# Three heads instead of two in a block-diagonal tile: the recurrent state of an mLSTM cell

## The chip, the cores and the metric

The kernel runs on one core of a Trainium2 chip. The metric is device time in microseconds (us), the median over several executions; lower is better. The engines meant below are TensorE (PE; its weight loads are listed apart as PEld), VectorE (DVE), ScalarE (ACT), GpSimd (POOL) and SyncE (SP), which here only issues transfers.

## The reference

An mLSTM cell is followed by a feed-forward block. There are 4 batches (B), 8 heads (H), 768 time steps (S) and a head dimension of 40 (D). The cell is a recurrence over time with a matrix state C and a vector state n for each batch and head:

```
m_new  = max(f + m, i)
f_stab = exp(f + m - m_new);  i_stab = exp(i - m_new)
C = f_stab * C + i_stab * v k^T
n = f_stab * n + i_stab * k
y = sigmoid(o) * (C q) / max(|n q|, 1)
```

The outputs y of all heads, 8 x 40 = 320 numbers per time step, form the rows x of a matrix of 3072 tokens. The block then computes `h = x @ w_in` (320 x 2048), `g = h - tanh(h)` and `g @ w_out` (2048 x 320). All of it is float32.

## The kernel before, in words

**Units and chunks.** Time is cut into 6 chunks of 128 steps. A unit is one chunk of one batch, all 8 heads of it, so there are 24 units (NU); unit n has chunk c = n // 4 and batch b = n % 4. Two units make a group of 256 tokens for the feed-forward block, which takes its 16 blocks of 128 hidden features in pairs.

**What a unit does.** The recurrence is written chunk by chunk. Within a chunk, a head's output is a masked product of scores with values (`scores`, then a mask on VectorE that writes P, then `intra`: one matmul per head, `ph<-vs,P`). What came before the chunk enters through the state: `inter` multiplies q by the state and starts the accumulation in the same PSUM tile `ph`. Units of the first chunk (0 to 3) have no state yet, so 20 of the 24 units have products with q. `gate` divides and applies the sigmoid, `turn` transposes the result with three matmuls (`px`), and ScalarE copies it to xT, the input of the feed-forward block. `update` forms k^T times the scaled values (`pc`), and `keep_state` adds the old state and multiplies by the decay on VectorE: new = (pc + old) * decay. The last four units update nothing, so 20 units have updates too. The values have a 41st column (D1 = D + 1) that carries the normaliser n along.

**The tile of two heads.** The state of a batch is a tile of 80 rows (TOP = 2 * D, line 283; the tiles at line 498). Heads 2j and 2j + 1 form pair j. Rows 0 to 39 belong to the even head, rows 40 to 79 to the odd one, and the columns hold 41 for each head. The two diagonal blocks are the two states; the other two blocks must be zero. `update` computes the whole square of 80 by 82 in one matmul, cross terms included, and the decay tile eT (line 333) removes them: it holds exp of the summed log decays in the diagonal blocks and zeros elsewhere. `states` (line 422) fills eT with two exponentials and one multiplication by zero on ScalarE, in each of three calls. The summed log decays come from a matmul with a matrix `ones` of TOP columns (line 319). Because the state is block-diagonal, one matmul of `inter` with q of two heads stacked in 80 rows (the tile q2) gives the outputs of both heads side by side: 128 rows of time, 2 x 41 columns.

In the trace a tile named q2 is shown as q. The float32 matmuls stand there as two records each, each with a weight load of its own. The first operand after the arrow in `ph<-state,q` is the one that is streamed, the second the one that is loaded as weights: for `inter` q2 is loaded (128 columns) and the state is streamed (82 columns); for `update` k is loaded (80 columns) and the scaled values are streamed (82 columns).

**Loads.** `load_unit` (line 287) issues a unit's transfers on SP, in order: kz and qz (q and k for the scores, two transfers each, one per half of the partitions), v, k, o and, if there is a state, q2 (two transfers, one for each 40 rows). k, q2 and most others have 3 buffers, so unit n's transfer waits until unit n - 3 has used its buffer.

**What sets the order of the work.** Every instruction on TensorE, VectorE and ScalarE is pinned behind the one written before it. For units 0 to 11 and the first feed-forward items a planner (class Plan, line 157) decides the order: each piece of work has an engine, an estimated time, what it comes after and a rank; the planner takes what can start first by its own clock, and of equals that with the lower rank. In it the second part of a unit (`inter` and `intra`) is four pieces, one per pair, of 0.43 us each with a state and 0.29 without; the updates of a unit are one piece of 0.55 us in which all four matmuls stand in a row (line 918 and the lines after). From unit 12 on the order is fixed by spreading: `cell_slot` (line 621) lists the steps of a unit, and `merge` (line 822) places them at even distances among the matmuls of the feed-forward block. So `inter`, `intra` and `update` stand there one at a time between wide matmuls (`ph_up`, 256 columns streamed, and `pS`, 160).

At the end of the kernel a conditional part (line 1237) repeats everything in a more general way if some values exceed a bound. In this execution it isn't entered: none of its instructions is in the trace.

Of the kernel before, what the change touches and what calls it, by code (L numbers as in the profile page):

```python
# [59 lines left out]
L = 128  # L60
# [18 lines left out]
def kernel(  # L79
# [200 lines left out]

    TOP = 2 * D

    ld = {}

    def load_unit(n, names=("kz", "qz", "v", "k", "o", "q2"), queue=nc.sync):
        c, b = divmod(n, B)
        t = ld.setdefault(n, {})
        for name in names:  # L290
            if name in ("kz", "qz"):
                t[name] = load.tile([128, HH, L], FP, name=name, tag=name, bufs=3)
                for i in range(2):
                    src = kT if name == "kz" else qT
                    queue.dma_start(out=t[name][i * HALF:i * HALF + D], in_=src[b, c, :, slice(i, H, 2)])
            elif name != "q2":
                src, bufs = {"v": (v, 3), "k": (k, 3), "o": (o_gate, 4)}[name]
                t[name] = load.tile([L, H, D], FP, name=name, tag=name, bufs=bufs)
                queue.dma_start(out=t[name], in_=src[b, c])
            elif c:  # L300
                t["q2"] = load.tile([TOP, HH, L], FP, name="q2", tag="q2", bufs=3)
                for i in range(2):
                    queue.dma_start(out=t["q2"][i * D:(i + 1) * D], in_=qT[b, c, :, slice(i, H, 2)])

    for n in range(2):
        load_unit(n, ("kz",))
# [23 lines left out]
    make_identity(nc, ident)  # L330
    V.memset(ones, 1.0)

    eT = const.tile([TOP, NU, HH, 2], FP, name="eT")
    G.memset(eT, 0.0)

    G.memset(upto, 1.0)
# [46 lines left out]
    def gate_columns(c0, c1, bank):  # L383

        cs = slice(c0, c1)
        some = CHUNKS.index(c0)
        least = sums[:, NS + some:NS + some + 1]

        def turned(i, row):
            p = bank(i, [L, NT, BH])  # L390
            for c in range(c0, c1):
                T.transpose(p[:, c, :], row[:, c * L:(c + 1) * L], ident[0:BH, 0:BH])
            return p[:, cs]

        def sums_of(i, w):
            p = bank(i, [w.shape[1], NT, BH])
            T.matmul(p[:, cs].rearrange("p c n -> p (c n)"), w, lfT[:, cs].rearrange("p c n -> p (c n)"),
                     start=True, stop=True)
            return p[:, cs]

        got = {}

        def forget():
            got["lf"] = turned(0, lf)

        def admit():
            got["i"] = turned(1, i_sb)

        def since():
            got["since"] = sums_of(0, upto)  # L410

        def whole():
            got["whole"] = sums_of(1, ones).rearrange("p c (b j two) -> p (c b) two j", two=2, j=HH)

        us = slice(c0 * B, c1 * B)

        def bounded():
            V.tensor_single_scalar(inv[:, cs], got["since"], 2 * DEEP, op=OP.max)
            V.tensor_reduce(out=least, in_=inv[:, cs].rearrange("p c n -> p (c n)"), axis=mybir.AxisListType.X, op=OP.min)
            V.tensor_single_scalar(least, least, TINY / DEEP, op=OP.mult)  # L420

        def states():
            A.activation(out=eT[:, us, :, 1], in_=got["whole"][:, :, 1, :], func=AF.Exp)
            A.activation(out=eT[0:D, us, :, 0], in_=got["whole"][0:D, :, 0, :], func=AF.Exp)
            A.mul(out=eT[0:D, us, :, 1], in_=eT[0:D, us, :, 1], mul=0.0)

        return {
            "forget": forget, "admit": admit, "since": since, "whole": whole,
            "lf": lambda: V.tensor_copy(out=lfT[:, cs], in_=got["lf"]),
            "i": lambda: A.activation(out=ei[:, 1, cs], in_=got["i"], func=AF.Exp),  # L430
            "bounded": bounded,
            "inverse": lambda: A.activation(out=inv[:, cs], in_=inv[:, cs], func=AF.Exp, scale=-1.0),
            "over": lambda: V.tensor_tensor(out=ei[:, 0, cs], in0=ei[:, 1, cs], in1=inv[:, cs], op=OP.mult),
            "states": states}
# [60 lines left out]

    part = [const.tile([L, DM], FP, name=f"part{i}") for i in range(FIRST * GT)]
    ys = [const.tile([L, DM], FP, name=f"ys{i}") for i in range(2)]
    state = [[const.tile([TOP, HH, 2, D1], FP, name=f"state{b}_{i}") for i in range(2)] for b in range(B)]

    un = {}  # L500

    def pair(t, j):

        return t[:, 2 * j:2 * j + 2].rearrange("p two d -> p (two d)")

    def arrive(n):
        t = un.setdefault(n, {})
# [59 lines left out]
    def inter(n, j):  # L567
        t = un[n]
        if "ph" not in t:
            t["ph"] = small([L, H, D1], "ph")  # L570
        if t["c"]:
            T.matmul(pair(t["ph"], j), t["qs"][:, j, :], pair(state[t["b"]][t["c"] % 2].rearrange("p j two d -> p (j two) d"), j), start=(j == 0), stop=False,
                     skip_group_check=True)

    def intra(n, h):
# [16 lines left out]
    def update(n, j, at_once=True):  # L592
        t = un[n]
        if j == 0:
            t["pc"] = small([TOP, HH, 2, D1], "pc")
        T.matmul(t["pc"][:, j].rearrange("p two d -> p (two d)"), pair(t["k"], j), pair(t.get("vs_end", t["vs"]), j), start=True, stop=True)
        if j == HH - 1 and at_once:
            keep_state(n)

    def keep_state(n):  # L600
        t = un[n]
        old, new = (state[t["b"]][(t["c"] + i) % 2].rearrange("p j two d -> p (j two) d") for i in range(2))
        pc = t["pc"].rearrange("p j two d -> p (j two) d")
        decay = eT[:, n].rearrange("p j two -> p (j two)").unsqueeze(2).to_broadcast([TOP, H, D1])
        if t["c"]:
            V.tensor_tensor(out=new, in0=pc, in1=old, op=OP.add)
        V.tensor_tensor(out=new, in0=new if t["c"] else pc, in1=decay, op=OP.mult)
# [13 lines left out]
    def cell_slot(s, o):  # L621
# [8 lines left out]
            begin(s)  # L630
        if o is None:
            return [(0.0, lambda: prepare(s))]
        for d in range(HH):
            steps.append((0.22 if o >= B else 0.0, lambda d=d: inter(o, d)))
            steps += [(0.22, lambda h=h: intra(o, h)) for h in (2 * d, 2 * d + 1)]
        steps.append((0.0, lambda: gate(o)))
        steps += 5 * pause
        if o + B < NU:
            steps += [(0.18, lambda j=j: update(o, j)) for j in range(HH)] + 4 * pause
        steps += [(0.11, lambda j=j: turn(o, j)) for j in range(NK + 1)] + 2 * pause  # L640
        if s is not None:
            steps.append((0.0, lambda: prepare(s)))
# [275 lines left out]
    def plan_unit(n, rank):  # L918
# [41 lines left out]
        def second_part(j):  # L960
            banks[:] = [held["small"]]
            inter(n, j)
            for h in (2 * j, 2 * j + 1):
                intra(n, h)

        for j in range(HH):
            op = plan.add("T", 0.43 if c else 0.29, lambda j=j: second_part(j), [op] if op else [*u["mask"], u["prep"], u["column"], *before, *of(n, "q2") * (c > 0)], rank,
                          take=() if op else [("small", held)], give=[("P", held)] if j == HH - 1 else ())
        u["second"] = op
        u["gate"] = plan.add("V", 1.5, lambda: gate(n), [op, u["open"], *of(n - 2, "turn")], rank, give=[("small", held)])  # L970

# [1 line left out]

        def updates():
            banks[:] = [held_c["small"]]
            for j in range(HH):
                update(n, j, at_once=False)

        def turns():
# [198 lines left out]
    def begin_any(n):  # L1178
# [7 lines left out]
                             op0=OP.mult, op1=OP.add)  # L1186
        t["decays"] = True
        if t["c"]:
            t["qs"] = att.tile([128, HH, L], FP, name="qs", tag="P", bufs=4)[0:TOP]
            for i in range(2):  # L1190
                spread(t["qs"][i * D:(i + 1) * D], g_rows, n, slice(i, H, 2))
            V.tensor_tensor(out=t["qs"], in0=t["qs"], in1=t["q2"], op=OP.mult)

    def keep_any(n):

        t = un[n]
        old, new = (state[t["b"]][(t["c"] + i) % 2] for i in range(2))
        decay = eT[:, n].unsqueeze(3).to_broadcast([TOP, HH, 2, D1])

        own = att.tile([TOP, HH, 2, D1], FP, name="own", tag="P", bufs=4)  # L1200
        V.memset(own, 1.0)
        V.memset(own[0:D, :, 1], 0.0)
        G.affine_select(out=own[:, :, 0], in_=own[:, :, 0], compare_op=OP.is_ge, fill=0.0, base=D - 1,
                        pattern=[[0, HH], [0, D1]], channel_multiplier=-1)
        V.tensor_tensor(out=own, in0=t["pc"], in1=own, op=OP.mult)
        if t["c"]:
            V.tensor_tensor(out=new, in0=old, in1=decay, op=OP.mult)
            V.tensor_tensor(out=new, in0=new, in1=own, op=OP.add)
        else:
            V.tensor_copy(out=new, in_=own)  # L1210
# [26 lines left out]
    with tc.If(nc.values_load(again, min_val=0, max_val=128,  # L1237
# [18 lines left out]
        for g in range(NG):  # L1256
            for n in range(g * GT, (g + 1) * GT):
# [3 lines left out]
                un[n]["vs_end"] = scaled(n, 1, "vs_end", 1)  # L1261
                un[n]["column"]()
                halves(scores(n))
                for j in range(HH):
                    inter(n, j)
                for h in range(H):
                    intra(n, h)
                gate(n)
                if n + B < NU:
                    for j in range(HH):  # L1270
                        update(n, j, at_once=False)
                    keep_any(n)
                for j in range(NK + 1):
# [58 lines left out]
```

## Time and profile before

| what | value |
|---|---|
| median of 3 runs | 565.8 us (565.06 to 565.92) |
| the profiled execution, first to last instruction (its span) | 559.5 us |
| TensorE clock granted, mean | 0.997 |
| TensorE busy; weight loads | 546.4 us; 461.2 us |
| VectorE busy | 346.0 us |
| ScalarE busy | 179.3 us |
| records of products with q, `ph<-state,q` | 160 |
| records of updates, `pc<-vs,k` | 160 |
| first and last product with q start | 59.4 us; 484.0 us (weight load; matmul) |
| first and last update start | 34.1 us; 406.4 us (weight load; matmul) |

The profile is of one execution, whose own time is known only as its span; what lies between it and the median of the runs, 6.3 us, is what precedes the first and follows the last instruction, together with the difference of one execution from another. A group of instructions in it is shown as line, engine, operation, output <- inputs, partitions x elements of each form and how many; then busy time in us and the mean of one in ns; then the idle time just before them and what ended it. Line 129 is the helper through which all matmuls go, line 133 the same for transposes, line 106 that for VectorE and ScalarE; so tiles, not lines, tell operations apart. In a timeline a row is start in us, length in us, engine, line, operation and tiles, and how many were merged. A matmul's length holds its latency, so the pace is read from one start to the next. A row of the table by stage is a stretch (from:to and its length), then busy us and count of PE, PEld, DVE, ACT and POOL, the clock, the busy share of the DMA engines and GB/s.

### The profile page before, as it was taken

Reading aid. Unit: us, or ns where it says so; the run is one execution under the profiler, and the core shown is the slowest. Engines: PE = TensorE matmul, PEld = TensorE weight load, DVE = VectorE, ACT = ScalarE, POOL = GpSimd, SP = SyncE. Lnnn points to the kernel's source line nnn. Section 1 sums busy time; section 2 is a strip of 40 time slices with the busy share of each in tenths; the row PEclk is TensorE's granted clock in tenths of the full one; section 3 lists DMA queues with packets and bytes.
Section 4 is the critical chain, followed back from the end, with each engine's and each line's share of the span. In section 5 each row is a group of like instructions: output and inputs, shape, how many; then the busy total and the mean of one; then the engine's idle time right before and its main releaser. Section 6 shows DMA issues by size and latency. Waiting matters only on the chain.

```text
span 559.5 us, 9108 instructions
## 1 busy us (share of the span) xinstructions
PE 546.4 (98%) x3460; PEld 461.2 (82%) x3460; DVE 346.0 (62%) x754; ACT 179.3 (32%) x441; POOL 34.3 (6%) x67
## 2 busy tenths in 40 slices
PE   7999999999999999999999999999999999999995
PEld 4767978787877777798898999989989989988873
DVE  4699888989854335767656647547556546553421
ACT  2344652443432312322232142133123123131321
POOL 6142030500000000000000000000000000000000
PEclk9999999999999999999999999999999999999998
DMA  7786353632210001201202112121110000000000
GB/s 217 216 260 215 119 171 91 183 113 94 83 36 1 0 1 54 77 23 49 84 25 60 57 41 69 48 83 49 58 37 13 0 25 2 2 25 0 25 0 29
DMA packets 40194, 38.21 MB, mean 68 GB/s; under 512 B 3856, under 2 KB 37712, under 8 KB 40144
## 3 DMA queue, kind: packets, MB, share of 16 engines
q1 hardware_dynamic: 32712, 22.49, 13.7%
q0 software_dynamic: 3296, 10.82, 6.1%
q10 hardware_dynamic: 4136, 4.26, 2.2%
q8 instruction: 29, 0.48, 0.3%
q14 instruction: 21, 0.17, 0.1%
HBM read 33.62 MB, written 3.93 MB: 67 GB/s over the span
## 4 chain that ended last, share of the span: by engine, by line
PE 95%; DVE 2%; DMA 1%; issue 0%; SPq 0%; ACT 0%
PE ph_up L129 40%; PE pS L129 20%; PE po L129 15%; PE ph L129 10%; PE ps L129 4%; PE pc L129 2%; PE px L133 2%; DMA kz<-in_kT 1%; DVE gt L106 1%; PE awake L129 0%; DVE P L106 0%; DVE w_e L106 0%; DVE w_in L106 0%; PE gate L129 0%; DVE den L106 0%
## 5 line engine op out<-in xcount | busy, mean ns | idle before, releaser
L129 PE MATMUL ph_up<-xT,w_in 128*128 128x256 f32 (+1 forms) x1152 | 248.9, 394 | 1.2 <-DVE gt L106 0.8
L129 PEld LDWEIGHTS ph_up<-xT,w_in 128*128 128x128 f32 (+1 forms) x1152 | 170.4, 190 | 34.3 <-issue 13.0
L106 ACT ACTIVATE z<-ph_up 128x512 f32<-128x512 f32 (+1 forms) x100 | 57.1, 576 | 283.4 <-issue 153.3
L106 DVE SCALAR_TENSOR_TENSOR gt<-ph_up,z 128x512 f32<-128x512 f32 (+1 forms) x100 | 63.4, 663 | 92.8 <-ACT z L106 92.5
L129 PE MATMUL po<-w_out,gt 128*128 128x320 f32 x320 | 93.9, 439 | 0.0
L129 PEld LDWEIGHTS po<-w_out,gt 128*128 128x128 f32 x320 | 58.5, 190 | 25.7 <-issue 5.0
L106 DVE TENSOR_TENSOR P<-ps,upto 128x512 f32<-128x512 f32 x48 | 31.6, 684 | 70.4 <-PE ps L129 70.4
L106 ACT ACTIVATE q<-z,tiny 128x512 f32<-128x512 f32 (+1 forms) x100 | 64.8, 701 | 0.0
L106 DVE SCALAR_TENSOR_TENSOR gt<-q,gt 128x512 f32<-128x512 f32 (+1 forms) x100 | 63.2, 662 | 2.0 <-ACT q L106 2.0
L129 PEld LDWEIGHTS ph<-vs,P 128*128 128x128 f32 x384 | 60.5, 202 | 4.7 <-issue 1.2
L129 PE MATMUL ph<-vs,P 128*128 128x41 f32 x384 | 59.7, 272 | 0.0
L129 PE MATMUL pS<-wT,s 128*128 128x160 f32 x336 | 52.0, 301 | 0.0
L129 PEld LDWEIGHTS pS<-wT,s 128*128 128x128 f32 x336 | 47.4, 190 | 0.0
L129 PE MATMUL pS<-w_out,gt 128*128 128x160 f32 x224 | 43.7, 315 | 0.0
L129 PEld LDWEIGHTS pS<-w_out,gt 128*128 128x128 f32 x224 | 32.7, 191 | 4.0 <-issue 3.0
L129 PE MATMUL ps<-qz,kz 40*128 40x128 f32 x384 | 30.1, 297 | 1.2 <-DMA kz<-in_kT 1.2
L129 PE MATMUL ph<-state,q 80*128 80x82 f32 x160 | 31.2, 276 | 0.0
L129 PEld LDWEIGHTS ps<-qz,kz 40*128 40x128 f32 x384 | 27.4, 205 | 4.1 <-issue 2.7
L129 PEld LDWEIGHTS ph<-state,q 80*128 80x128 f32 x160 | 26.4, 191 | 2.7 <-issue 0.7
L448 POOL DMA_DIRECT2D w<-in_moe_w_in x40 | 22.5, 566 | 52.9 <-DVE w_e L106 43.2
L106 ACT COPY xT<-px 128x384 f32<-128x384 f32 x24 | 11.4, 476 | 39.6 <-PE px L133 39.6
L129 PEld LDWEIGHTS pc<-vs,k 128*80 128x80 f32 x160 | 17.9, 150 | 4.8 <-DVE state L106 0.7
(90 smaller groups left out, 443.5 us busy)
## 6 DMA issues: line engine op xcount, KB each, us to landing
w<-in_moe_w_out POOLq DMA_DIRECT2D x16, 320.0 KB, 3.6
kz<-in_kT SPq DMA_DIRECT2D x48, 80.0 KB
o<-in_o_gate SPq DMA_DIRECT2D x24, 160.0 KB
k<-in_k SPq DMA_DIRECT2D x24, 160.0 KB
out<-ob ACTq DMA_DIRECT2D x24, 160.0 KB
qz<-in_qT SPq DMA_DIRECT2D x44, 80.0 KB
v<-in_v SPq DMA_DIRECT2D x22, 160.0 KB
q<-in_qT SPq DMA_DIRECT2D x40, 80.0 KB
```

The costliest lines, as they stand in the source:

```text
L106: i = method(*args, **kwargs)
L129: return cls.keep(nc.tensor.matmul(*args, **kwargs))
L133: return cls.keep(nc.tensor.transpose(*args, **kwargs))
L448: queue.dma_start(out=to[rows, cols], in_=part)
```

## The change

The heads are grouped in threes: heads 0 to 2, 3 to 5, and 6 and 7. The state tile has 120 rows and its columns are head by head as before; the blocks on the diagonal of each trio (40 rows by 41 columns) are the states. `inter` becomes three matmuls: q of up to three heads stacked in 120 rows (80 for the last) as weights, and 123, 123 and 82 columns of state streamed. `update` becomes three matmuls that load 120 columns of k each. For the last trio there are only two heads, so the tile of k is widened to nine heads; its transfer reads 360 numbers per row, the last 40 of which belong to the next row, and the rows of `pc` that come from them meet a zero decay. The k of the last four units, which no update reads, is no longer loaded.

q2 comes in three transfers, of 3, 3 and 2 heads of 40 rows. eT takes three exponentials and two multiplications by zero instead of two and one; the matrix of ones has 120 columns. In the planner the second part is three pieces of 0.575, 0.575 and 0.43 us (0.435, 0.435 and 0.29 without a state). The piece of the updates is left at 0.55 us. In the merged part `inter` of a trio is followed by the three `intra` of its heads, and the three updates are entered at 0.2 us each.

The conditional part is changed likewise (its own mask of the diagonal blocks, its spreading of decays over q2) and is left out here.

```diff
-    TOP = 2 * D
+    TRIO = 3
+    TOP = TRIO * D
+    WIDE = -(-H // TRIO) * TRIO
+    TRIOS = [range(h, min(h + TRIO, H)) for h in range(0, H, TRIO)]
...
+            elif name == "k":
+                if n + B < NU:
+                    t["k"] = load.tile([L, WIDE, D], FP, name="k", tag="k", bufs=3)
+                    queue.dma_start(out=t["k"].rearrange("p h d -> p (h d)"),
+                                    in_=bass.AP(k.tensor, k[b, c].offset, [[H * D, L], [1, WIDE * D]]))
             elif name != "q2":
-                src, bufs = {"v": (v, 3), "k": (k, 3), "o": (o_gate, 4)}[name]
+                src, bufs = {"v": (v, 3), "o": (o_gate, 4)}[name]
...
             elif c:
-                t["q2"] = load.tile([TOP, HH, L], FP, name="q2", tag="q2", bufs=3)
-                for i in range(2):
-                    queue.dma_start(out=t["q2"][i * D:(i + 1) * D], in_=qT[b, c, :, slice(i, H, 2)])
+                t["q2"] = load.tile([TOP, len(TRIOS), L], FP, name="q2", tag="q2", bufs=3)
+                for i in range(TRIO):
+                    queue.dma_start(out=t["q2"][i * D:(i + 1) * D, 0:len(range(i, H, TRIO))], in_=qT[b, c, :, slice(i, H, TRIO)])
...
-    eT = const.tile([TOP, NU, HH, 2], FP, name="eT")
+    eT = const.tile([TOP, NU, H], FP, name="eT")
...
         def states():
-            A.activation(out=eT[:, us, :, 1], in_=got["whole"][:, :, 1, :], func=AF.Exp)
-            A.activation(out=eT[0:D, us, :, 0], in_=got["whole"][0:D, :, 0, :], func=AF.Exp)
-            A.mul(out=eT[0:D, us, :, 1], in_=eT[0:D, us, :, 1], mul=0.0)
+            for i in reversed(range(TRIO)):
+                rows, heads = slice(0, (i + 1) * D), slice(i, H, TRIO)
+                A.activation(out=eT[rows, us, heads], in_=got["whole"][rows, :, heads], func=AF.Exp)
+                if i:
+                    A.mul(out=eT[0:i * D, us, heads], in_=eT[0:i * D, us, heads], mul=0.0)
...
-    state = [[const.tile([TOP, HH, 2, D1], FP, name=f"state{b}_{i}") for i in range(2)] for b in range(B)]
+    state = [[const.tile([TOP, H, D1], FP, name=f"state{b}_{i}") for i in range(2)] for b in range(B)]
...
-    def pair(t, j):
-
-        return t[:, 2 * j:2 * j + 2].rearrange("p two d -> p (two d)")
+    def trio(t, j):
+
+        return t[:, TRIOS[j].start:TRIOS[j].stop].rearrange("p h d -> p (h d)")
...
         if t["c"]:
-            T.matmul(pair(t["ph"], j), t["qs"][:, j, :], pair(state[t["b"]][t["c"] % 2].rearrange("p j two d -> p (j two) d"), j), start=(j == 0), stop=False,
+            rows = slice(0, len(TRIOS[j]) * D)
+            T.matmul(trio(t["ph"], j), t["qs"][rows, j, :], trio(state[t["b"]][t["c"] % 2][rows], j), start=(j == 0), stop=False,
                      skip_group_check=True)
...
-            t["pc"] = small([TOP, HH, 2, D1], "pc")
-        T.matmul(t["pc"][:, j].rearrange("p two d -> p (two d)"), pair(t["k"], j), pair(t.get("vs_end", t["vs"]), j), start=True, stop=True)
-        if j == HH - 1 and at_once:
+            t["pc"] = small([TOP, H, D1], "pc")
+        T.matmul(trio(t["pc"], j), t["k"][:, TRIO * j:TRIO * (j + 1)].rearrange("p h d -> p (h d)"), trio(t.get("vs_end", t["vs"]), j), start=True, stop=True)
+        if j == len(TRIOS) - 1 and at_once:
             keep_state(n)
...
-        for d in range(HH):
+        for d, heads in enumerate(TRIOS):
             steps.append((0.22 if o >= B else 0.0, lambda d=d: inter(o, d)))
-            steps += [(0.22, lambda h=h: intra(o, h)) for h in (2 * d, 2 * d + 1)]
+            steps += [(0.22, lambda h=h: intra(o, h)) for h in heads]
...
-            steps += [(0.18, lambda j=j: update(o, j)) for j in range(HH)] + 4 * pause
+            steps += [(0.2, lambda j=j: update(o, j)) for j in range(len(TRIOS))] + 4 * pause
...
-        for j in range(HH):
-            op = plan.add("T", 0.43 if c else 0.29, lambda j=j: second_part(j), [op] if op else [*u["mask"], u["prep"], u["column"], *before, *of(n, "q2") * (c > 0)], rank,
-                          take=() if op else [("small", held)], give=[("P", held)] if j == HH - 1 else ())
+        for j, heads in enumerate(TRIOS):
+            op = plan.add("T", 0.145 * len(heads) + (0.14 if c else 0.0), lambda j=j: second_part(j), [op] if op else [*u["mask"], u["prep"], u["column"], *before, *of(n, "q2") * (c > 0)], rank,
+                          take=() if op else [("small", held)], give=[("P", held)] if j == len(TRIOS) - 1 else ())
```

More of the change, by code (lines that the diff above doesn't have):

```diff
@@ L412, in whole @@
         def whole():
-            got["whole"] = sums_of(1, ones).rearrange("p c (b j two) -> p (c b) two j", two=2, j=HH)
+            got["whole"] = sums_of(1, ones).rearrange("p c (b h) -> p (c b) h", h=H)
         us = slice(c0 * B, c1 * B)
@@ L601, in keep_state @@
         t = un[n]
-        old, new = (state[t["b"]][(t["c"] + i) % 2].rearrange("p j two d -> p (j two) d") for i in range(2))
-        pc = t["pc"].rearrange("p j two d -> p (j two) d")
-        decay = eT[:, n].rearrange("p j two -> p (j two)").unsqueeze(2).to_broadcast([TOP, H, D1])
+        old, new = (state[t["b"]][(t["c"] + i) % 2] for i in range(2))
+        pc = t["pc"]
+        decay = eT[:, n].unsqueeze(2).to_broadcast([TOP, H, D1])
         if t["c"]:
@@ L962, in second_part @@
             inter(n, j)
[L963 removed]
+            for h in TRIOS[j]:
                 intra(n, h)
[L966 to L968 removed]
+        for j, heads in enumerate(TRIOS):
+            op = plan.add("T", 0.145 * len(heads) + (0.14 if c else 0.0), lambda j=j: second_part(j), [op] if op else [*u["mask"], u["prep"], u["column"], *before, *of(n, "q2") * (c > 0)], rank,
+                          take=() if op else [("small", held)], give=[("P", held)] if j == len(TRIOS) - 1 else ())
         u["second"] = op
@@ L975, in updates @@
             banks[:] = [held_c["small"]]
-            for j in range(HH):
+            for j in range(len(TRIOS)):
                 update(n, j, at_once=False)
@@ L1188, in begin_any @@
         if t["c"]:
[L1189 to L1192, printed above, removed]
+            t["qs"] = att.tile([128, len(TRIOS), L], FP, name="qs", tag="P", bufs=4)[0:TOP]
+            for i in range(TRIO):
+                spread(t["qs"][i * D:(i + 1) * D, 0:len(range(i, H, TRIO))], g_rows, n, slice(i, H, TRIO))
+            for j, heads in enumerate(TRIOS):
+                rows = slice(0, len(heads) * D)
+                V.tensor_tensor(out=t["qs"][rows, j], in0=t["qs"][rows, j], in1=t["q2"][rows, j], op=OP.mult)
     def keep_any(n):
@@ L1197, in keep_any @@
         old, new = (state[t["b"]][(t["c"] + i) % 2] for i in range(2))
-        decay = eT[:, n].unsqueeze(3).to_broadcast([TOP, HH, 2, D1])
-        own = att.tile([TOP, HH, 2, D1], FP, name="own", tag="P", bufs=4)
+        decay = eT[:, n].unsqueeze(2).to_broadcast([TOP, H, D1])
+        own = att.tile([TOP, H, D1], FP, name="own", tag="P", bufs=4)
         V.memset(own, 1.0)
-        V.memset(own[0:D, :, 1], 0.0)
-        G.affine_select(out=own[:, :, 0], in_=own[:, :, 0], compare_op=OP.is_ge, fill=0.0, base=D - 1,
-                        pattern=[[0, HH], [0, D1]], channel_multiplier=-1)
+        for i in range(TRIO):
+            heads = slice(i, H, TRIO)
+            pattern = [[0, len(range(i, H, TRIO))], [0, D1]]
+            if i:
+                V.memset(own[0:i * D, heads], 0.0)
+            if i < TRIO - 1:
+                G.affine_select(out=own[:, heads], in_=own[:, heads], compare_op=OP.is_ge, fill=0.0, base=(i + 1) * D - 1,
+                                pattern=pattern, channel_multiplier=-1)
         V.tensor_tensor(out=own, in0=t["pc"], in1=own, op=OP.mult)
@@ L1263 @@
                 halves(scores(n))
-                for j in range(HH):
+                for j in range(len(TRIOS)):
                     inter(n, j)
@@ L1269 @@
                 if n + B < NU:
-                    for j in range(HH):
+                    for j in range(len(TRIOS)):
                         update(n, j, at_once=False)
```

## The prediction

> **What bounds the kernel now.** I read the page first (busy shares, chain), then the groups kept apart by shape, then TensorE's timeline in two stretches, then the table by stage and the waits of SP and ACT. The page:
>
> ```profile
> span 559.5 us, 9108 instructions
> PE 546.4 (98%) x3460; PEld 461.2 (82%) x3460; DVE 346.0 (62%) x754; ACT 179.3 (32%) x441; POOL 34.3 (6%) x67
> ...
> PE 95%; DVE 2%; DMA 1%; issue 0%; SPq 0%; ACT 0%
> ```
>
> TensorE holds 95% of the chain that ended last. A matmul's "busy" is latency as well as work, so I don't price with it. The groups by shape tell what there is to change; each fp32 matmul stands as two records, each with its own weight load:
>
> ```profile
> L129 PE MATMUL ph<-state,q 80*128 80x82 f32 x160 | 31.2, 276 | 0.0
> L129 PE MATMUL pc<-vs,k 128*80 128x82 f32 x160 | 19.0, 237 | 0.5 <-DVE state L106 0.5
> ...
> L129 PEld LDWEIGHTS ph<-vs,P 128*128 128x128 f32 x384 | 60.5, 202 | 4.7 <-issue 1.2
> L129 PEld LDWEIGHTS ph<-state,q 80*128 80x128 f32 x160 | 26.4, 191 | 2.7 <-issue 0.7
> L129 PEld LDWEIGHTS pc<-vs,k 128*80 128x80 f32 x160 | 17.9, 150 | 4.8 <-DVE state L106 0.7 <-issue 0.3
> ```
>
> 160 records are 20 units of 4 pairs of heads. What a record costs is read from start to start. Where the order was planned (units 0 to 11) these matmuls stand in a row:
>
> ```profile
> 89.86 0.43 PE L129 MATMUL ph<-state,q 80*128 80x82 f32 x2
> 90.13 0.58 PE L129 MATMUL ph<-vs,P 128*128 128x41 f32 x4
> 90.53 0.43 PE L129 MATMUL ph<-state,q 80*128 80x82 f32 x2
> ...
> 97.21 0.49 PE L133 MATMUL px<-ident,ys 128*128 128x128 f32 x3
> 97.54 0.74 PE L129 MATMUL pc<-vs,k 128*80 128x82 f32 x8
> 98.11 1.28 PE L129 MATMUL po<-w_out,gt 128*128 128x320 f32 x4
> ```
>
> Six records of ph take 0.67 us, 0.112 each, though four of them stream only 41 columns: the load of 128 weight columns sets the pace, not the stream. px, 128 columns loaded and 128 streamed, takes 0.33 / 3 = 0.11: a stream of 128 still fits under a load of 128. pc, 80 loaded and 82 streamed, takes 0.57 / 8 = 0.071. In the merged part (units 12 to 23) they stand singly among wide matmuls:
>
> ```profile
> 403.62 1.03 PE L129 MATMUL ph_up<-xT,w_in 128*128 128x256 f32 x4
> 404.49 0.30 PE L129 MATMUL pc<-vs,k 128*80 128x82 f32 x2
> 404.63 0.64 PE L129 MATMUL ph_up<-xT,w_in 128*128 128x256 f32 x2
> 405.10 0.30 PE L129 MATMUL pc<-vs,k 128*80 128x82 f32 x2
> ...
> 413.21 0.35 PE L129 MATMUL ph<-state,q 80*128 80x82 f32 x2
> 413.39 1.07 PE L129 MATMUL ph_up<-xT,w_in 128*128 128x256 f32 x4
> 414.30 0.31 PE L129 MATMUL ph<-vs,P 128*128 128x41 f32 x2
> ```
>
> Four wide records alone take 404.49 - 403.62 = 0.87; with one product with q before them 414.30 - 413.21 = 1.09, so that product costs 0.22, again 0.11 a record. One update with two wide records takes 405.10 - 404.49 = 0.61; less 0.43, an update costs 0.18.
>
> The table by stage (busy time per engine, clock, DMA share) says whether freed TensorE time reaches the end:
>
> ```profile
> 40.00:60.00 20.00, 19.50 (x144) 16.02 (x145) 19.66 (x42) 11.14 (x28) 5.14 (x10) 1.00 0.66 205
> 80.00:100.00 20.00, 20.00 (x145) 16.31 (x144) 15.99 (x36) 8.80 (x22) 1.10 (x2) 1.00 0.39 117
> 228.00:420.00 192.00, 191.22 (x1361) 172.94 (x1357) 119.55 (x272) 52.87 (x139) 0.00 (x0) 1.00 0.18 53
> ```
>
> Until 60 us VectorE is as full as TensorE (19.66 of 20). From 60 us on VectorE has 10 to 38% free, and the list of waits names a single one of TensorE's matmuls between 60 and 486 us, 0.8 us on VectorE's gt at 231. The first product with q starts at 59.66 us: all of them lie where TensorE is the bound.
>
> **What the Trainium skill says.** "TensorE: Matmul & The Clock Gate", section "LDWEIGHTS (loading the stationary operand)": the load's time goes with the columns and not with the contraction rows. The trace agrees: 191 ns with 80 rows, 190 to 202 with 128, but 150 with 80 columns. Same page, "Back-to-back issue gap": in a stream of load and matmul pairs both set the spacing; the 0.112 and 0.071 us above agree. "VectorE: DVE Perf Modes", "Why `tensor_reduce` can't reduce along partition axis": the partitions are independent lanes, so 120 rows should cost what 80 do; the state's 80x328 operation takes 0.49 us and the one that makes vs on 128x320 0.48. "Perfetto Trace Analysis", section "What “DMA-bound” means": the window of an issue on SP is the making of descriptors. The trace has 0.76 us for half of a q2 (40 partitions of 4 heads) and 0.33 to 0.43 for a k.
>
> **The change part by part.**
>
> Products with q. 4 become 3 per unit: 20 units x 1 matmul x 2 records x 0.112 = -4.48 us. Those that stay load 128 columns as before; 40 more rows cost nothing (above), and 123 columns streamed lie below px's 128, so they stay at 0.112. The intra-chunk products are regrouped, not changed. Bounds: -4.4 (0.11 a record), and for a stream that does show see the second rival.
>
> State updates. 3 matmuls, each loading 120 columns (the last too, over a ninth head of padding) and streaming 123, 123, 82. No row shows that shape; from px, 0.11 at most and 0.11 x 120 / 128 = 0.103 at least; I take 0.105. In a row, units 0 to 11: 6 x 0.105 = 0.63 against 0.57, 12 x 0.06 = +0.72. Singly, units 12 to 19: 3 x 0.215 = 0.645 against 4 x 0.18 = 0.72, 8 x -0.075 = -0.60. Together +0.1 (bounds -0.1 to +0.6).
>
> The sums with ones: 6 records load 120 columns for 80, 40 x 0.11 / 128 = 0.034 each; four before 12 us, where TensorE waits for kz until 8.72 us. +0.1.
>
> VectorE: the update adds and scales the same 328 columns, 0. No instruction is added to it.
>
> ACT: eT takes 3 exponentials and 2 multiplications in place of 2 and 1, three times. Three instructions took 6.88 to 7.21 us and 12.26 to 12.60, so +0.22 each. At 7 us the reciprocal bound and "over" behind it come later, and VectorE is idle until 10.48. At 12.3 the column of ones for unit 0 moves from 12.91 to 13.1, and TensorE comes to it at 14.16. At 55.8 the second square moves from 56.19 to 56.45 and ends by 57.2; VectorE takes it up at 57.59. 0, and at most 3 x 0.25 if the cover failed.
>
> SP: q2 comes in three transfers for two, 20 issues more, packets and bytes alike. At 0.43 (by packets) to 0.76 us each; only three fall where SP has no free time, 20.7 to 43.1 us, behind them kz, qz, v, k and the gates: 1.3 to 2.3 us late. The least cover there: qz of unit 3 issued by 23.9, used at 38.5; k of unit 1 issued by 25.4, used at 44.5; the second gate rows by 24.9, scanned at 47.9; over 14 us each. q2 itself is issued 20 us ahead. 0. A k of 1,440 bytes a row for 1,280 adds 20 KB, 7 x 20 KB before 60 us, 0.65 us of the transfers at 219 GB/s, under the same cover; the last four k, which nothing reads, fall away.
>
> The planner: a unit's second part is entered at 0.575 + 0.575 + 0.43 = 1.58 in place of 4 x 0.43 = 1.72, in steps of three heads; until the first product with q its sums are the old ones (1.16). Afterwards the written order can differ. I take 0, with +-1 us in the range.
>
> Sum: -4.48 + 0.1 + 0.1 = -4.3 us. The profiled span goes from 559.5 to 555.2. The median of the runs, 565.8, lies 6.3 above the span (start and end of the launch, and the spread of 0.9); I carry it over: **561.5 us**, -0.8%.
>
> **The rivals.** A measurement here tells 0.2%, 1.1 us, from no change.
>
> VectorE takes over in the planned part. There 8 units save 8 x (0.224 - 0.06) = 1.3 us; if the masks, sums and conversions, 80 to 90% of VectorE, can't come earlier, this is lost: 562.8, up to 563.4 with the early +0.7. Against: TensorE shows no wait there.
>
> The stream shows. Starts read alone give the product with q 0.27 for two records, 0.135 each, and the intra ones 0.10. If that is its price and it goes with columns, 123 of them cost 0.135 + 41 x 0.11 / 128 = 0.17: 120 x 0.17 = 20.4 against 160 x 0.135 = 21.6, -1.2, with the +0.2 a time of 564.8, no change. Against: singly it cost 0.11, and px has 0.11.
>
> Slower: the new written order makes TensorE wait. Place: units 4 to 11, 59.7 to 156 us, where TensorE follows the order as planned and a mask's turn on VectorE can come after the products that need it. Price: a pair of masks, 1.27 us in the chain at 228.4. It decides from four such waits (4.3 / 1.27 = 3.4); ten would give about 570, five 567.8. For: VectorE is at 80 to 90%, and the planner enters 1.58 for what takes 22 x 0.112 = 2.5. Against: it was as far off before (1.72 for 2.7), and not one such wait is in this stretch. The same freedom can also close the 0.8 us at 231: 560.7.
>
> **How the numbers follow.** Forecast 0.70 (its own range 560.3 to 562.6), VectorE 0.10, stream 0.07, waits 0.08, lucky order 0.05. Faster: 0.70 + 0.10 + 0.05 = 0.85; same 0.07; slower 0.08. The range 560.0 to 564.2 takes in the first two and most of the last.
>
> **What would show it.** Right: ph<-state,q with 120 records, still 0.67 + 0.22 = 0.89 us for 8 records of a trio in a row; pc<-vs,k with 120 at 0.10 to 0.11; weight loads of state,q near 190 ns; slots of the merged part about 0.3 us shorter than the 21.65 between its recurring scores (289.57 to 311.21); TensorE's waits from 60 to 486 us still about 1 us. Wrong: products with q over 0.12 a record, new waits of TensorE on VectorE's P or gt, or on the q2 transfers.

## The result, and the profile after

The kernel with three heads in a tile takes 556.18 us (555.52 to 556.96), the kernel before it 565.43 us beside it: ratio 0.9848, 95% interval 0.983 to 0.9866. That is 9.2 us gained where 4.3 were forecast, and it lies below the range. The profiled execution of after has a span of 553.7 us, 5.8 less than that of before. So already the two views disagree on the gain by 3.4 us.

The page of after (span, busy time, the chain that ended last by engine):

```profile
span 553.7 us, 8979 instructions
PE 539.0 (97%) x3378; PEld 455.6 (82%) x3380; DVE 345.7 (62%) x754; ACT 179.8 (32%) x447; POOL 34.2 (6%) x67
...
PE 91%; DMA 4%; DVE 3%; issue 1%; SPq 0%; ACT 0%; POOL 0%; DVEq 0%; ACTq 0%
```

TensorE still holds the chain. (Most of the 4% of DMA is one stretch from 32 to 45 us; a second profile of the same kernel has PE 93% and DMA 1%.) The groups of after, kept apart by shape, have 120 records in place of 160 each for the products with q and the updates:

```profile
L129 PE MATMUL ph<-state,q 120*128 120x123 f32 x80 | 16.1, 283 | 0.0
L129 PE MATMUL ph<-state,q 80*128 80x82 f32 x40 | 8.2, 286 | 0.0
L129 PE MATMUL pc<-vs,k 128*120 128x123 f32 x80 | 13.7, 276 | 0.5 <-DVE state L106 0.5
```

TensorE's timeline of after, in a row (first three lines) and singly (the others):

```profile
88.46 0.46 PE L129 MATMUL ph<-state,q 120*128 120x123 f32 x2
88.76 0.76 PE L129 MATMUL ph<-vs,P 128*128 128x41 f32 x6
89.35 0.43 PE L129 MATMUL ph<-state,q 80*128 80x82 f32 x2
...
307.83 1.06 PE L129 MATMUL ps<-qz,kz 40*128 40x128 f32 x16
314.49 0.37 PE L129 MATMUL pc<-vs,k 128*120 128x123 f32 x2
315.14 0.37 PE L129 MATMUL pc<-vs,k 128*120 128x123 f32 x2
329.09 1.06 PE L129 MATMUL ps<-qz,kz 40*128 40x128 f32 x16
```

The same two rows before the change:

```profile
311.04 1.06 PE L129 MATMUL ps<-qz,kz 40*128 40x128 f32 x16
332.68 1.06 PE L129 MATMUL ps<-qz,kz 40*128 40x128 f32 x16
```

A trio's eight records take 89.35 - 88.46 = 0.89 us, as forecast: here 123 columns streamed add nothing to a load of 128. A single update with its two wide records takes 315.14 - 314.49 = 0.65, so 0.22 for the update (0.215 forecast). A slot of the merged part, from scores to scores, is 329.09 - 307.83 = 21.26 us against 332.68 - 311.04 = 21.64 before. On what the matmuls cost the forecast held. The rest had to be found elsewhere.

### The profile page after: what moved, and what is told of

The parts are those of the page before. It is cut to its first block, busy times and chain, and to the rows that moved or that the text cites. A ratio compares the mean times of both kernels' runs of the same rounds, so it can differ in the third digit from the quotient of the medians.

```text
span 553.7 us, 8979 instructions
## 1 busy us (share of the span) xinstructions
PE 539.0 (97%) x3378; PEld 455.6 (82%) x3380; DVE 345.7 (62%) x754; ACT 179.8 (32%) x447; POOL 34.2 (6%) x67
## 4 chain that ended last, share of the span: by engine, by line
PE 91%; DMA 4%; DVE 3%; issue 1%; SPq 0%; ACT 0%; POOL 0%; DVEq 0%; ACTq 0%
PE ph_up L129 38%; PE pS L129 20%; PE po L129 15%; PE ph L129 9%; PE ps L129 4%; PE pc L129 2%; PE px L133 2%; DMA v<-in_v 1%; DMA kz<-in_kT 1%; DMA q<-in_qT 1%; DVE P L106 1%; DVE w_e L106 1%; DMA w<-in_moe_w_in 0%; DVE gt L106 0%; DVE state L106 0%
## 5 line engine op out<-in xcount | busy, mean ns | idle before, releaser
L129 PE MATMUL ph_up<-xT,w_in 128*128 128x256 f32 (+1 forms) x1152 | 245.4, 391 | 2.1 <-DVE w_in L106 1.3
L129 PEld LDWEIGHTS ph_up<-xT,w_in 128*128 128x128 f32 (+1 forms) x1152 | 169.8, 189 | 35.1 <-issue 12.7
L129 PEld LDWEIGHTS po<-w_out,gt 128*128 128x128 f32 x320 | 58.4, 190 | 26.4 <-issue 5.0
L129 PE MATMUL pS<-w_out,gt 128*128 128x160 f32 x224 | 40.4, 310 | 0.0
L129 PEld LDWEIGHTS pS<-w_out,gt 128*128 128x128 f32 x224 | 32.7, 194 | 1.3 <-issue 1.0
L129 PE MATMUL ph<-state,q 120*128 120x123 f32 (+1 forms) x120 | 24.3, 284 | 0.0
L129 PEld LDWEIGHTS ph<-state,q 120*128 120x128 f32 (+1 forms) x120 | 19.9, 191 | 1.5
L106 DVE TENSOR_TENSOR s<-gt 128x256 f32<-128x256 f32 x56 | 21.1, 417 | 0.0
```

Source lines behind the costliest of these rows:

```text
L106: i = method(*args, **kwargs)
L129: return cls.keep(nc.tensor.matmul(*args, **kwargs))
```

## The experiments

Three theories stood at first. "Records": the gain is the weight loads saved, at 0.112 us a record. "Ends": something outside the span went away, the unread transfers of k for instance. "Spread": before has executions that its one profile doesn't show. Each run's median is compared with executions of before on the same chip, taken beside it.

**The kernel before again.** No edit.

> The kernel before, unchanged, to learn how its own executions spread and what lies around the span. The kernel after has 1.8 us between device time and span (555.5 against 553.7). If before has the same, its usual span is near 563.6 us, its profiled execution with 559.5 was a quick one, and a second profile should show where 4 us can differ between executions (theory 'spread'). If its spans repeat 559.5, before has 5.9 us outside the span and after 1.8, and the change has taken 4 us away at the ends of the launch (theory 'ends'). Ratio to before 1.000 either way.

Measured: 564.69 us over 22 executions, 559.35 to 568.18, ratio 0.9995 (0.9974 to 1.0016). In every one of them the device time is 1.7 to 1.9 us above the span; so "ends" falls, and the 559.5 of the first profile was a quick execution. This run's own profile, with a span of 562.9, shows what the others have. Its table by stage (the clock is the third number from the end):

```profile
60.00:64.00 4.00, 4.00 (x44) 3.83 (x42) 2.88 (x9) 0.73 (x3) 0.00 (x0) 1.00 0.21 59
64.00:68.00 4.00, 4.00 (x26) 4.00 (x25) 1.84 (x5) 2.17 (x4) 0.00 (x0) 0.62 0.49 150
68.00:72.00 4.00, 4.00 (x16) 3.43 (x17) 2.29 (x7) 1.07 (x2) 0.00 (x0) 0.53 0.15 42
```

The first profile, with its span of 559.5, has the full clock in the same place and 37 and 29 matmul records there in place of 26 and 16:

```profile
64.00:68.00 4.00, 4.00 (x37) 3.86 (x37) 2.88 (x10) 2.62 (x5) 0.00 (x0) 1.00 0.50 152
68.00:72.00 4.00, 4.00 (x29) 3.07 (x28) 3.96 (x7) 2.63 (x7) 0.00 (x0) 1.00 0.52 153
```

TensorE's timeline in this run:

```profile
64.52 0.59 PE L129 MATMUL ph<-vs,P 128*128 128x41 f32 x4
64.92 0.87 PE L133 MATMUL px<-ident,ys 128*128 128x128 f32 x3
65.58 0.56 PE L129 MATMUL ph<-state,q 80*128 80x82 f32 x2
65.93 0.99 PE L129 MATMUL ph<-vs,P 128*128 128x41 f32 x4
66.72 0.70 PE L129 MATMUL ph<-state,q 80*128 80x82 f32 x2
```

TensorE was busy without a gap, and yet its granted clock fell to one half at 65 us and came back at 72: four intra-chunk records that took 64.92 - 64.52 = 0.40 us just before take 66.72 - 65.93 = 0.79 behind it. It happens after 5 us of products with q and intra-chunk products of units 4 and 5, with the scores of unit 6 between them. Half of about 7 us is 3.4 us lost. Every profile ends with 1.6 to 4.4 us at half clock, so a mean of 0.996 to 0.999 is that of an execution without a halving on the way. Of all 151 executions of before in these comparisons, 129 had a mean granted clock of 0.993 or less, with a median of 564.8 us; only 19 had 0.996 or more, with a median of 560.7. The first profile (0.997) was of the rare kind. Where the clock fell is known for this one profile of before alone; 39 of the 151 have a mean of 0.987 or less, which is an estimated 0.013 x 563 / 0.5 = 15 us at half clock, less at most 4.4 at the end, so more than this one stretch.

**The unread transfers of k.**

```diff
+                if name == "k" and n + B >= NU:
+                    continue
                 t[name] = load.tile([L, H, D], FP, name=name, tag=name, bufs=bufs)
```

> The kernel before, with only the last four transfers of k left out, which no instruction reads. Theory 'ends': the unread transfers cost time outside the span or hold SP, so 561.5 to 562.5. My forecast's step: they cost nothing, 565.4, ratio 1.000.

Measured: 564.37 us, ratio 1.000 (0.9971 to 1.0029). They cost nothing. Its profile happened to have no halving (span 557.5, clock 0.997) and serves below as the undisturbed picture of before. It is 2.0 us shorter than the first profile, which had no halving either: here TensorE came to its full clock at 25.4 us and to the first product with q at 57.7, there at 30.9 and 59.7; in the profile of after the full clock came at 25.3 us. So of the 5.8 us between the first two profiled spans, 2.0 belong to the start and 3.8 to the change.

**One product with q given back.** In `inter`, for the first trio:

```diff
+            one = slice(0, 2 * D1) if j == 0 else slice(0, len(TRIOS[j]) * D1)
-            T.matmul(trio(t["ph"], j), t["qs"][rows, j, :], trio(state[...][rows], j), ...)
+            T.matmul(trio(t["ph"], j)[:, one], t["qs"][rows, j, :], trio(state[...][rows], j)[:, one], ...)
+            if j == 0:
+                two = slice(2 * D1, 3 * D1)
+                T.matmul(trio(t["ph"], j)[:, two], t["qs"][rows, j, :], trio(state[...][rows], j)[:, two], ...)
```

> The kernel after, with the first trio's product with q given back as two matmuls over the same weights (82 and 41 columns streamed), so 4 per unit again. If a product costs two weight loads of 0.112 us wherever it stands: 20 x 0.224 = +4.5 us on after, 560.7. If the products matter less and the gain came from elsewhere: below +2, under 558.

Measured: 561.71 us, ratio 0.9969 (0.9948 to 0.9991): 5.5 to 5.8 above after. Of 22 executions 17 had a clock of 0.996 to 0.998, with a median of 561.2; 5 had 0.991 and about 564.5. The price of a product holds roughly (5.0 to 5.3 where 4.5 was expected; before at full clock differs by 0.8 between this chip and that of the second run of after, 560.8 and 560.0), and the lower clock is back in part. The forecast of this run, 560.7, was 1.0 too low.

**One update given back**, the same way: the first trio's update in two matmuls that load the same 120 columns and stream 82 and 41.

> The kernel after, with the first trio's update given back as two matmuls (120 columns loaded twice, 82 and 41 streamed). If the loads of 120 columns set the pace, 0.104 a record in a row and about 0.11 singly: 20 x 0.21 = +4.2 us, 560.4. If the stream sets it: 41 columns more of start-up only, below +1.5, under 557.7.

Measured: 560.52 us, ratio 0.9925 (0.9904 to 0.9947), 4.3 to 4.6 above after: the load of 120 columns sets the pace. All 14 executions kept 0.996 or more.

So the records explain some 4.3 us, and the new theory is "clock": in before, what TensorE does near 65 us brings the halving on, and the change removes the cause. Two forms of before test it. Neither saves a matmul.

**Wide: a third head of zeros behind each pair.** The state tile gets a third block of columns, zeroed once, the tile `ph` gets room for a ninth head (`t["wide"]`), and `inter` streams all three blocks:

```diff
-    state = [[const.tile([TOP, HH, 2, D1], FP, name=f"state{b}_{i}") for i in range(2)] for b in range(B)]
+    wide = [[const.tile([TOP, HH, 3, D1], FP, name=f"state{b}_{i}") for i in range(2)] for b in range(B)]
+    state = [[t[:, :, 0:2, :] for t in two] for two in wide]
...
-            T.matmul(pair(t["ph"], j), ...)
+            T.matmul(t["wide"][:, 2 * j:2 * j + 3].rearrange("p h d -> p (h d)"), t["qs"][:, j, :], wide[...][:, j].rearrange("p h d -> p (h d)"), ...)
```

> The kernel before with a third head of zeros streamed behind each pair: 123 columns a product for 82, still 4 products a unit, same loads, so no TensorE time should be gained or lost at full clock (560.7, the median of those executions of before whose mean granted clock was 0.997). Theory 'clock': what TensorE does in a stretch decides whether its clock is halved; columns streamed in the rows of ph go from 41 to 51% of the time, so the halvings near 65 us should go and the median come to about 561, ratio 0.994. Theory 'order': halvings come from the number and order of instructions; then they stay, 564.3, ratio 1.000.

Measured: 561.08 us, ratio 0.9931 (0.991 to 0.9953). None of 16 executions was below 0.994. More work, and 4 us less time. TensorE's timeline shows that the wider stream itself is free:

```profile
58.42 0.46 PE L129 MATMUL ph<-state,q 80*128 80x123 f32 x2
58.72 0.54 PE L129 MATMUL ph<-vs,P 128*128 128x41 f32 x4
59.09 0.46 PE L129 MATMUL ph<-state,q 80*128 80x123 f32 x2
```

Six records in 59.09 - 58.42 = 0.67 us, to the hundredth what they took with 82 columns.

**Tall: 40 rows of zeros under each pair.** The state tile and q2 get 120 rows, the last 40 of the state being zeros; `inter` contracts over all of them.

```diff
-    state = [[const.tile([TOP, HH, 2, D1], FP, name=f"state{b}_{i}") for i in range(2)] for b in range(B)]
+    tall = [[const.tile([3 * D, HH, 2, D1], FP, name=f"state{b}_{i}") for i in range(2)] for b in range(B)]
+    state = [[t[0:TOP] for t in two] for two in tall]
...
-                for i in range(2):
+                for i in range(3):
-                    queue.dma_start(out=t["q2"][i * D:(i + 1) * D], in_=qT[b, c, :, slice(i, H, 2)])
+                    queue.dma_start(out=t["q2"][i * D:(i + 1) * D], in_=qT[b, c, :, slice(i % 2, H, 2)])
```

> The kernel before with the products with q contracted over 120 rows, 40 of them zeros in the state (a third transfer fills q2), 82 columns as before. No time at full clock either (560.7). If the columns streamed decide about the clock (41%, as before): 564.3. If the part of the array in use decides, rows times columns (82x80 of 128 rows was 33% of the time, 82x120 is 39.5%): about 561, as for the wide form, whose share is 39.5% too. If neither: 564.3.

Measured: 562.68 us, ratio 0.9977 (0.9958 to 0.9996). 18 of 22 executions had 0.994 or more, at about 562.6; 4 had 0.985. At full clock that is about 2 us more than before; zeroing the large tiles takes VectorE 2.8 us at the start (first product with q at 61.49 us in its profile), so a control was needed.

**Tall off.** The same zeroing and transfers, contracted over 80 rows: `t["qs"][0:TOP, j, :]` and `state` in that matmul.

> The control of the 120-row form: the same zeroing of the state tiles and the same third transfer of q2, but the product is contracted over 80 rows again. If the rows in use are what kept the clock there (4 of 22 executions below 0.99, against most of before), the halvings return: most executions at 0.983 to 0.992, and a median 3 to 4 us above the 562.7 of the 120-row form, about 566. If it was only the shift in time that the zeroing brings, the clock stays as there and the median is 562.7.

Measured: 565.88 us, ratio 1.0062 (1.0036 to 1.0088). All 19 executions had 0.993 or less. In its profile the clock is halved twice: from 29.3 to 32.7 us, just after a wait of TensorE of 1.92 us, and without any wait in units 6 and 7, at 94 us:

```profile
92.00:96.00 4.00, 4.00 (x30) 4.00 (x30) 2.01 (x7) 0.85 (x2) 0.00 (x0) 0.77 0.22 69
96.00:100.00 4.00, 4.00 (x26) 3.70 (x27) 2.56 (x7) 0.00 (x0) 0.00 (x0) 0.50 0.27 81
```

So 40 rows of zeros in the streamed operand, which change no result and no pace, keep the clock up in most executions.

**The kernel after again**, without an edit.

> The kernel after, unchanged, for the spread of its clock, of which only four executions are known, all at 0.997. Theory 'clock': nearly all at 0.996 to 0.998, median 556.2, ratio 0.985 to 0.986; if the four were luck, a part at 0.991 and below with 3 to 5 us more, median 557 to 560.

Measured: 555.92 us (555.75 to 556.48), ratio 0.9849 (0.9808 to 0.989); all five executions had 0.997 or 0.998. With the first four that is none of nine.

Put together, for the products of one whole unit in a row, worked out: a column streamed is 0.215 / 256 = 0.84 ns, a record 0.112 us, and the array in use weighs each column with its rows of 128. Before, a unit streams 8 x 82 + 16 x 41 = 1312 columns in 24 records, 1.10 of 2.69 us; after, the same 1312 in 22 records.

| kernel | columns streamed, share of time | array in use, share of time | executions with a clock under 0.994 | median us |
|---|---|---|---|---|
| before, tall off | 41% | 33% | 129 of 151, 19 of 19 | 564.0 to 565.9 |
| one product given back | 41% | 38% | 5 of 22 | 561.7 |
| tall | 41% | 40% | 4 of 22 | 562.7 |
| wide | 51% | 40% | 0 of 16 | 561.1 |
| after | 45% | 42% | 0 of 9 | 556.2, 555.9 |

The columns alone don't sort the kernels (41% stands beside three different outcomes); the part of the array in use does. The other four forms of after that are tried here, which all keep the trios' products with q, have none under 0.994 in 30 executions. That the array in use is what the clock goes by is a reading of five points, three of them within 38 to 40%, not more. Wide and tall leave the number and the pace of the records as they are, so these don't explain the clock there; for after itself the shorter stretch (22 records for 24) wasn't tested apart.

**The planner's order.** In after, the estimate of the second part is put back to the sum of before:

```diff
-            op = plan.add("T", 0.145 * len(heads) + (0.14 if c else 0.0), ...
+            op = plan.add("T", 0.145 * len(heads) + (0.187 if c else 0.0), ...
```

> The kernel after with the planner's sum for the second part put back to the 1.72 us of before (0.622, 0.622 and 0.477), so that units 6 and 7 stand in a row again and one transposition of unit 5 moves back between its products. My forecast's step: the order is worth 0 with +-1 us, 555 to 557. If the order and not the columns streamed kept the clock full, halvings come back: executions at 0.991 and below, median over 558.

Measured: 555.19 us (553.96 to 556.58), ratio 0.9868 (0.982 to 0.9916), all six executions at 0.996 or 0.998. The order of before is not what loses the clock. What the new order costs in time lies within the spread (555.2 against 555.9 and 556.2, with ranges that overlap). The profiles of the two kernels, which came to the full clock at 25.4 and 25.3 us, differ by 0.2 us (553.5 against 553.7), and that of after has a wait of this size at the scores of unit 9 that neither before nor this kernel has:

```profile
106.63 1.16 PE L129 MATMUL ps<-qz,kz 40*128 40x128 f32 x14 [0.21 <-DVE P L106]
```

**A faster version.** If use of the array brings the clock up, the start can gain too. `intra` of units 0 to 3 streams three heads for one; the two that don't belong are overwritten by the products behind.

```diff
+        hs = slice(h, min(h + TRIO, H)) if t["c"] == 0 else slice(h, h + 1)
-        T.matmul(t["ph"][:, h, :], t["P"][:, h % 2, h // 2, :], t["vs"][:, h, :], start=(t["c"] == 0 and h == 0), ...
+        T.matmul(t["ph"][:, hs, :].rearrange("p h d -> p (h d)"), t["P"][:, h % 2, h // 2, :], t["vs"][:, hs, :].rearrange("p h d -> p (h d)"),
+                 start=(t["c"] == 0), ...
```

> The kernel after with the intra-chunk products of units 0 to 3 streaming three heads of values, 123 columns for 41 (the two that don't belong are overwritten by the products behind them); loads of 128 columns set their pace, so nothing is added at a given clock. TensorE's clock became full at 25.3 us in the profile of after. If the columns streamed bring the full clock, it comes before 22 us, and the scores of unit 2 and the products of unit 1 run at the full pace: -1 to -2 us on after, 554.2 to 555.2. If not: 556.2.

Measured: 553.52 us (553.18 to 554.57), ratio 0.9811 (0.9769 to 0.9852), 2.4 below after on the same chip, more than the 1 to 2 expected. Unit 1 and the scores of unit 2 in after:

```profile
19.00 3.47 PE L129 MATMUL ph<-vs,P 128*128 128x41 f32 x16
25.18 1.18 PE L129 MATMUL ps<-qz,kz 40*128 40x128 f32 x16
```

and in this kernel:

```profile
18.00 1.87 PE L129 MATMUL ph<-vs,P 128*128 128x123 f32 x16
22.45 1.16 PE L129 MATMUL ps<-qz,kz 40*128 40x128 f32 x16
```

Three times the columns in about half the time. The full clock came at 17.7 us in this profile. Both edits in one kernel:

> The kernel after with both edits that made it faster alone: three heads streamed in units 0 to 3 (553.5) and the planner's sum back at 1.72 us (555.2 against 555.9). If the earlier full clock and the order of units 4 to 11 are independent: 552.8. If the planner's order rests on the early times, which the plan doesn't know: the 0.7 is lost, 553.5.

Measured: 552.38 us (551.73 to 553.62), ratio 0.9799 (0.9775 to 0.9823). That is 3.5 to 3.8 us below after, and the lowest median of all that ran. Its profile came to the full clock at 16.5 us and doesn't have the wait at the scores of unit 9. That the second edit adds to the first isn't shown: the two runs were on different chips, and their ratios overlap.

## Why the prediction was right or wrong

**The direction and the price of the work were right; the clock was left out.** TensorE was the bound, weight loads set the pace, and what was forecast for the work is what an undisturbed comparison gives: executions of before at full clock have a median of 560.7, after has 555.9 and 556.2, so 4.5 to 4.8 us against 4.3 (4.0 where the second run of after stands beside four such executions of before).

**Products with q**, -4.48: right. 0.89 us for a trio's eight records, and a product given back costs 5.0 to 5.3 us at full clock. The rival of a stream that shows falls with the 0.67 us of the wide form.

**Updates**, +0.1: right as nearly nothing; the sign isn't settled. Singly 0.22 as forecast; in a row six take 33.60 - 33.00 = 0.60 in the profile of after where I put 0.63:

```profile
33.00 0.76 PE L129 MATMUL pc<-vs,k 128*120 128x123 f32 x6
33.60 0.38 PE L129 MATMUL awake<-diag 128*128 128x512 bf16 x1
```

With these prices and those of before, 12 x (0.60 - 0.57) - 8 x (0.72 - 0.66) = -0.1, at the edge of the bounds.

**VectorE, ACT, SP**, 0: right as far as the profiles show. The state's operation takes 0.49 us on 120 rows as on 80. After has two waits of weight loads that before doesn't have, 0.2 us each, one of scores on a transfer of q2 and one on eT; no matmul shows a wait on either. SP's three issues of q2 have a median of 0.34 us each, 1.0 in all against 1.5 for two before, less than my lower bound.

**The planner**, 0 +- 1: right; the one loss that a profile shows is a wait on VectorE's P, the sign of being wrong that the prediction names, but of 0.2 us and not 1.27. By stage, undisturbed before (557.5) against after (553.7):

| stretch | before | after | difference | forecast |
|---|---|---|---|---|
| to the first product with q | 57.7 | 58.4 | +0.7 | +0.3 |
| to the scores of unit 12 | 167.6 | 166.9 | -0.7 | -1.3 |
| to the scores of unit 23 | 233.3 | 229.8 | -3.5 | -3.1 |
| to the end | 98.9 | 98.6 | -0.3 | -0.2 |

The +0.7 is there from the first 13 us on: the scores of unit 1 start at 12.7 us against 11.8. The slots, 21.64 us before (the prediction has 21.65), gained 0.38 us where 0.30 was counted; what the other 0.08 is I didn't trace.

Two more figures of the prediction are wrong, without a part in the result: ten waits of 1.27 us would have made 574 us, not 570; and VectorE's free share goes up to 58% (160 to 228 us, 28.47 busy of 68), not 38%.

**The step that failed is the last of the sum**: "The median of the runs, 565.8, lies 6.3 above the span (start and end of the launch, and the spread of 0.9); I carry it over". What lies outside the span is 1.7 to 1.9 us in every execution. The other 4.4 us were time inside the span that the profiled execution didn't have: a lower clock of TensorE, in 129 of 151 executions, which in the one of them that was profiled halved for 6.8 us after the dense row of small products. It was no constant, and with the change it is gone (0 of 9). That the change did this by using more of the array is the reading of the table above, argued and not shown for after itself. The clock of 0.997 on the page made me take the clock as given; a distance of 6.3 us between a profile and its runs, whose own spread was 0.9, should have been a question and not a term. The prediction put a change of the clock at nothing without a reason; none of its rivals held this case, and the range ended 3.8 us above the result.

## What to carry to other kernels

Compare the profiled span with the timed runs before any sum is made: a distance that launch doesn't explain is time that this profile doesn't show. Where loads of weights set TensorE's pace, as the loads of 128 columns did here, streaming more columns (123 for 82 or 41) and contracting over more rows (120 for 80) cost no time in these runs, and were even worth it where they were zeros. A TensorE that is busy without a gap isn't safe from a lower clock; here a stretch of 5 us of small matmuls stood before it.

## What the runs showed of the hardware that I had not expected

- The granted clock fell to half within a stretch without idle time, for 6.8 us (64.95 to 71.78 in one profile, 94.14 to 100.96 in another), and whether it does differs from one execution of the same kernel to the next.
- In these two profiles the clock changes only at whole multiples of 3.41 us from one another: at 30.82, 64.95 and 71.78 in the first (10 and 2 of them), at 25.87, 29.28, 32.70, 94.14 and 100.96 in the second (1, 1, 18 and 2). How this raster lies to the work doesn't decide alone: the first profile of before (full clock at 30.88, first product with q at 59.66) kept the clock, that of the run without an edit (30.82 and 59.77) lost it.
- Zeros in the streamed operand count as use: 41 columns of zeros (0 of 16 executions below 0.994) or 40 rows of zeros (4 of 22) kept the clock that the same kernel without them loses (19 of 19 in the control).
- At the start the pace is half until 24.8 to 34.0 us in the eleven profiles with 41 columns in units 0 and 1, although TensorE works from 9 us on, in the profile of after almost without a gap; streaming 123 columns in their place brought the full pace to 17.7 and 16.5 us in the two profiles that have it. The page's row of the clock doesn't show this first stretch.
- An issue of a transfer of 40 partitions with three or two heads takes 0.34 us on SP (median of 60 in the profile of after), with four heads 0.76 (median of 40 in that of before).
